# Attention rows in blocks of 128 with one block shared by two heads, and a rearranged start, in an attention-then-feed-forward kernel

## The chip, the cores and the metric

The kernel runs on one core of one Trainium2 chip. The metric is the time of one execution in microseconds of device time (us). A profile has its own span, from the first to the last instruction, which is about 2 us shorter than the time. Where differences are a few tenths of a microsecond, this document compares spans and single waits of the profiles, because the times of one kernel differ by more than that from run to run.

## The reference

```python
# q, k, v: (8 batches, 12 heads, 448 rows, 64); w_in 768 x 2048, w_out 2048 x 768
scores = q @ k.T / 8                       # per batch and head
attn = exp(scores - max) / sum
x = (attn @ v), heads side by side         # 3584 rows x 768
h = x @ w_in;  g = maximum(0.01 * h, h)
out = g @ w_out                            # float32
```

## The kernel before

Two heads of one batch make a "pair"; there are 48 pairs. TensorE (PE) forms transposed scores, ScalarE (ACT) takes exponentials into a buffer `e`, TensorE multiplies a block of rows of `e` by `v`, to which a column of ones is appended so that column 65 is the sum, VectorE (DVE) divides by it, and the result `x` is transposed into `xT` for the feed-forward layers. Attention of later pairs ("clusters") is woven between the feed-forward groups of earlier batches.

```python
SC = 112; NSC = 4                          # 448 rows = 4 blocks of 112
ps_s: 3 PSUM tiles of two banks (scores); ps_g: 2 PSUM tiles of one bank (all else)
v_sb = [v_pool.tile([SC, 2, NSC, D + 1], BF16, ...)]   # head, key chunk, 65 columns

def expo(u, c):                            # key chunk c of pair u, both heads
    e = e_sb[u % NE][:, :EL].rearrange("p (j c s) -> p j c s", j=2, c=NSC)
    nc.scalar.activation(e[:, :, c, :], sc_t.pop((u, c))[:SC, :, :S], AX.Exp, scale=scale)

def pv(u, j, bank=None):                   # head j of pair u: 16 products
    ...
    for qc in range(NSC):
        for c in range(NSC):
            at = (j * NSC + c) * S + qc * SC
            nc.tensor.matmul(ps[:, qc, :], e[:, at:at + P], vt[:, j, c, :],
                             start=(c == 0), stop=(c == NSC - 1))
    ...
    nc.vector.reciprocal(rec, ps[:SC, :, D:])
    nc.vector.tensor_mul(x_t[u][:, :, j, :], ps[:SC, :, :D], rec.to_broadcast([SC, NSC, D]))

def cluster(g):                            # r = g % 4, heads = one or two (pair, head)
    ...
    elif len(heads) > 1:
        pv(*heads.pop(0))                  # two heads: the first before the scores
    for a, c in chunks: scores(a, c)
    for a, c in chunks[:2]: expo(a, c)
    ...
    for a, j in heads:                     # one head: after the scores
        pv(a, j)
        if j == 1 and a >= NXP: x_transposes(a)     # a transposing DMA
```

This kernel loads stationary operands of 128 columns throughout, so a block of 112 rows is loaded with 16 columns of its neighbour, which are computed and thrown away.

The softmax here doesn't subtract the row's maximum and nothing guards it: scores larger than these inputs give would overflow.

Of the kernel before, what the change touches and what calls it, by code (L numbers as in the profile page):

```python
# [9 lines left out]
F32 = mybir.dt.float32  # L10
BF16 = mybir.dt.bfloat16
AX = mybir.ActivationFunctionType
# [4 lines left out]
def kernel(  # L17
# [9 lines left out]
    nc = tc.nc  # L27

    B, H, S, D = q.shape
    DM, DF = moe_w_in.shape  # L30
    P = 128
    HP = H // 2
    SC = 112
    NSC = S // SC
    KD = DM // P
    MD = DF // P
    NW = DM // 2
    NU = B * HP
    scale = 1.0 / float(D) ** 0.5
# [7 lines left out]
    ld_pool = ctx.enter_context(tc.tile_pool(name="ld", bufs=5))  # L47
# [2 lines left out]
    qk_pool = ctx.enter_context(tc.tile_pool(name="qk", bufs=1))  # L50
    exp_pool = ctx.enter_context(tc.tile_pool(name="exp", bufs=1))
    r_pool = ctx.enter_context(tc.tile_pool(name="rec", bufs=4))
    x_pool = ctx.enter_context(tc.tile_pool(name="x", bufs=3))
    xT_pool = ctx.enter_context(tc.tile_pool(name="xT", bufs=1))
    h_pool = ctx.enter_context(tc.tile_pool(name="h", bufs=2))
# [3 lines left out]
    ps_s = ctx.enter_context(tc.tile_pool(name="ps_s", bufs=3, space=PSUM))  # L59
    ps_g = ctx.enter_context(tc.tile_pool(name="ps_g", bufs=2, space=PSUM))  # L60


    NV = 5
    v_sb = [v_pool.tile([SC, 2, NSC, D + 1], BF16, name=f"v{i}") for i in range(NV)]

    NE = 3
    EL = 2 * NSC * S
    e_sb = [exp_pool.tile([SC, EL + P - SC], BF16, name=f"e{i}") for i in range(NE)]
# [6 lines left out]

    NX = 4 * S
    assert all(any(c == d for d in cuts) for c in range(0, B * S + 1, NX))
    xT = xT_pool.tile([P, KD, NX], BF16)

    w_in_sb = w_pool.tile([P, KD, DF], BF16)  # L80
    w_out_sb = w_pool.tile([P, MD, DM], BF16)
    w_in_v = moe_w_in.rearrange("(ko ki) n -> ki ko n", ki=P)
    w_out_v = moe_w_out.rearrange("(ko ki) n -> ki ko n", ki=P)

    raw = {}
    qk_sb = {}
# [3 lines left out]
    NSW = 18  # L90

    def half(t, i=None):

        t = t.rearrange("p h so d -> p (h so d)").bitcast(BF16)
        t = t.rearrange("p (u h so d) -> p u h so d", u=2, h=2, so=NSC)
        return t if i is None else t[:, i]

    def load_soft(u, n, which):
        b, hp = divmod(u, HP)
        for x in which:  # L100
            t = ld_pool.tile([SC, 2, NSC, D], F32, name="f" + "qkv"[x])
            nc.gpsimd.dma_start(
                out=half(t)[:, :n].rearrange("p u h so d -> p (u h) (so d)"),
                in_=(q, k, v)[x][b, 2 * hp:2 * hp + 2 * n].rearrange(
                    "h (p so) d -> p h (so d)", so=NSC),
            )
            for i in range(n):
                raw.setdefault(u + i, {})[x] = half(t, i)

    def load_one(u, x, queue):  # L110
        b, hp = divmod(u, HP)
        t = ld_pool.tile([SC, 2, NSC, D], F32, name="f" + "qkv"[x])
        queue.dma_start(
            out=t.rearrange("p h so d -> p h (so d)"),
            in_=(q, k, v)[x][b, 2 * hp:2 * hp + 2].rearrange("h (p so) d -> p h (so d)", so=NSC),
        )
        raw.setdefault(u, {})[x] = t

    def load(u):
        if u >= NU:  # L120
            return
        if u < NSW:
            if u % 2 == 0:
                load_soft(u, 2, (0, 1, 2))
            return
        for x in range(3):
            load_one(u, x, nc.sync)

    def cast(u, parts=(0, 1, 2), by=nc.gpsimd.tensor_copy):
        if u >= NU:  # L130
            return
        for x in parts:
            f = raw[u].pop(x)
            if u not in qk_sb:
                qk_sb[u] = cast_pool.tile([SC, 2, NSC, 2, D], BF16, name="qkb")
            if x < 2:
                by(qk_sb[u][:, x].rearrange("p so h d -> p h so d"), f)  # L137
            else:
                by(v_sb[u % NV][:, :, :, :D], f)  # L139
# [4 lines left out]
    for i in range(4):  # L144
        at = (slice(None), ts(i % 2, MD // 2), ts(i // 2, NW))
# [20 lines left out]
    warm = const_pool.tile([P, 512], BF16)  # L166
# [7 lines left out]
    def warm_up(n):  # L174
        for _ in range(n):
            ps = ps_g.tile([P, 512], F32, name="mm", tag="g")
            nc.tensor.matmul(ps, warm[:, :P], warm, start=True, stop=True)

    warm_up(8)
    for t in v_sb:  # L180
        nc.vector.memset(t[:, :, :, D:], 1.0)
# [1 line left out]
        nc.vector.memset(t[:, EL:], 0.0)  # L183
    for t in qkT:
        nc.vector.memset(t[:, QL:], 0.0)
    fast = nc.vector.tensor_copy

    cast(0, (1,), lambda o, i: (nc.scalar.copy(o[:, 0], i[:, 0]), fast(o[:, 1], i[:, 1])))
# [4 lines left out]
    x_t = {}  # L193
# [4 lines left out]
    def turn(dst, src):  # L198
        nc.sync.dma_start_transpose(out=dst.rearrange("p (c s) -> p c s", s=SC), in_=src)
# [15 lines left out]
    def transposes(u, bank=None):  # L215
        if u >= min(NPE, NU):
            return
        for parts in ((1,), (0,)) if u == 0 else ((0, 1),):
            tr = turn_tile(bank)
            for i in parts:  # L220
                for so in range(NSC):
                    nc.tensor.transpose(  # L222
                        tr[:, i, ts(so, SC)], qk_sb[u][:, i, so], ident[:SC, :SC]
                    )
            at = slice(parts[0], parts[-1] + 1)
            nc.vector.tensor_copy(  # L226
                qkT[u % NQ][:, :QL].rearrange("p (i s) -> p i s", i=2)[:, at], tr[:, at]
            )

    sc_t = {}  # L230
# [11 lines left out]
            )  # L242

    def expo(u, c):
        e = e_sb[u % NE][:, :EL].rearrange("p (j c s) -> p j c s", j=2, c=NSC)
        nc.scalar.activation(e[:, :, c, :], sc_t.pop((u, c))[:SC, :, :S], AX.Exp, scale=scale)  # L246

    def pv(u, j, bank=None):

        e, vt = e_sb[u % NE], v_sb[u % NV]  # L250
        if bank is None:
            ps = ps_g.tile([P, NSC, D + 1], F32, name="pv", tag="g")
        else:
            ps = bank[:, :NSC * (D + 1)].rearrange("p (q d) -> p q d", q=NSC)
        for qc in range(NSC):
            for c in range(NSC):
                at = (j * NSC + c) * S + qc * SC
                nc.tensor.matmul(  # L258
                    ps[:, qc, :], e[:, at:at + P], vt[:, j, c, :],
                    start=(c == 0), stop=(c == NSC - 1),  # L260
                )
        if j == 0:
            x_t[u] = x_pool.tile([SC, NSC, 2, D], BF16, name="x")
        rec = r_pool.tile([SC, NSC, 1], F32, name="rec")
        nc.vector.reciprocal(rec, ps[:SC, :, D:])  # L265
        nc.vector.tensor_mul(  # L266
            x_t[u][:, :, j, :], ps[:SC, :, :D], rec.to_broadcast([SC, NSC, D])
        )

    def x_transposes(u, bank=None):  # L270
        b, hp = divmod(u, HP)
        at = b * S % NX
        dst = xT[:, hp, at:at + S]
        if u >= NXP:
            turn(dst, x_t.pop(u).rearrange("p so h d -> p (so h d)"))
            return
        tr = turn_tile(bank)
        for so in range(NSC):
            nc.tensor.transpose(tr[:, 0, ts(so, SC)], x_t[u][:, so], ident[:SC, :SC])  # L279
        nc.vector.tensor_copy(dst, tr[:, 0, :])  # L280
# [24 lines left out]
    def part(i, m, kks, bank=None):  # L305
# [8 lines left out]
        for kk in kks:  # L314
            nc.tensor.matmul(  # L315
                open_t[m][:, :n], w_in_sb[:, kk, ts(m, P)], xT[:, kk, at:at + n],
                start=(fresh and kk == kks[0]), stop=(kk == KD - 1),
            )

    def mlp(i):  # L320
# [3 lines left out]
        if i == 0:  # L324
            for m in opened:
                part(i, m, (KD - 1,))
        for m in range(MD):
# [33 lines left out]

    def supply(u):

        for what, n in {0: [('qk', 2), ('v', 1), ('v', 2), ('load', 6)], 1: [('qk', 3), ('qk', 4), ('v', 3), ('w', 1)], 2: [('qk', 5), ('v', 4), ('v', 5), ('load', 8)], 3: [('qk', 6), ('v', 6), ('w', 1)], 4: [('qk', 7), ('v', 7), ('w', 1)], 5: [('qk', 8), ('v', 8), ('load', 10), ('w', 1)]}[u]:
            if what == "qk":
                cast(n, (0, 1), fast if n in (2, 3) else nc.gpsimd.tensor_copy)
            elif what == "v":
                cast(n, (2,))
            elif what == "load":
                load(n)  # L370
            else:
                load_w(n)

    def first(u):

        scores(u, 0)
        scores(u, 1)
        expo(u, 0)
        if u == 0:
            warm_up(2)  # L380
        expo(u, 1)
        if u == 0:
            scores(u, 2)
        if u >= 2:
            x_transposes(u - 2)
        if u >= 1:
            pv(u - 1, 0)
        if 0 < u < 2:
            scores(u, 2)
        transposes(u + 1)  # L390
        if u + 1 < HP:
            supply(u)
        if u >= 2:
            scores(u, 2)
        scores(u, 3)
        expo(u, 2)
        expo(u, 3)
        if u + 1 == HP:
            supply(u)
        if u >= 1:  # L400
            pv(u - 1, 1)


    def cluster(g):
# [35 lines left out]
    a, b = idle_slot()  # L440
# [23 lines left out]
    for i in range(B):  # L464
        work = list(range(begin[i], begin[i + 1])) if i + 1 < B else []
        n = cuts[i + 1] - cuts[i]
# [47 lines left out]
```

## Time and profile before

| | before |
|---|---|
| time, median of 3 runs | 416.49 us |
| span of the profile | 414.4 us |
| TensorE busy | 98% |
| attention-times-v products (line L258) | 1536, 13% of the chain that ended last |
| feed-forward products (L315, L349) | 70% of the chain |

The page's chain follows the work that ended last back from the end. A line with 13% there can give at most that. The lines themselves are in the prediction below.

How to read the lines of a profile: a timeline line gives the start and the duration in us, the engine, the line of kernel.py, the operation, the tile written and the tiles read, their shapes, how many instructions were merged, and in brackets how long the engine stood idle before and what ended that. PEld is TensorE's load of a stationary operand, which overlaps its products. PSUM is the memory that TensorE writes and VectorE and ScalarE read. A wait list gives total, number and longest; a DMA queue gives packets, megabytes and its share of the 16 DMA engines' time.

### The profile page before, as it was taken

The numbers are of one execution on the slowest core, as the hardware profiler recorded it, in microseconds if no ns is written. First come the engines' busy times: TensorE is split into PE (matmuls) and PEld (weight loads), VectorE is DVE, ScalarE is ACT, GpSimd is POOL, SyncE is SP. The second block draws the span as 40 slices with busy tenths as digits, with TensorE's granted clock in tenths as the row PEclk, the third lists the DMA queues.
The fourth block names the chain that finished last, engine by engine and source line by source line (L and its number), as shares of the span: only waits on it lengthen the run. The fifth ranks groups of instructions, "written<-read, shape, count | busy, mean of one in ns | idle before, by whom it ended". The sixth has DMA issues, their size and how long they took to land.

```text
span 414.4 us, 9008 instructions
## 1 busy us (share of the span) xinstructions
PE 405.9 (98%) x3758; PEld 235.8 (57%) x3758; DVE 104.0 (25%) x295; ACT 228.9 (55%) x324; POOL 105.6 (25%) x177
## 2 busy tenths in 40 slices
PE   7899999999999999999999999999999999999996
PEld 2566666554656665654565656554465666654564
DVE  3762432211323113220222212221032211320021
ACT  5988773567434774476633684467643587214300
POOL 8876656311212213130311221131130200000000
PEclk9999999999999999999999999999999999999999
DMA  9999999971866847593466947757274440230022
GB/s 133 196 201 204 202 199 129 234 186 46 178 164 175 172 114 178 140 223 100 112 161 168 205 113 182 194 149 191 77 169 132 120 58 15 60 89 0 0 78 77
DMA packets 96585, 57.23 MB, mean 138 GB/s; under 512 B 53280, under 2 KB 93088, under 8 KB 96544
## 3 DMA queue, kind: packets, MB, share of 16 engines
q1 hardware_dynamic: 76816, 44.12, 44.5%
q0 software_dynamic: 19392, 12.26, 20.6%
q8 instruction: 29, 0.48, 0.5%
q10 hardware_dynamic: 336, 0.28, 0.2%
q14 instruction: 12, 0.10, 0.1%
HBM read 45.61 MB, written 11.01 MB: 137 GB/s over the span
## 4 chain that ended last, share of the span: by engine, by line
PE 95%; DVE 2%; DMA 1%; ACT 1%; issue 0%; POOLq 0%
PE mm L349 35%; PE mm L315 35%; PE pv L258 13%; PE sc L237 10%; PE tr L222 1%; DMA fq<-in_q_dram 1%; ACT e L246 1%; PE tr L279 1%; DVE x L266 1%; PE sc L315 0%; DVE o L353 0%; DVE qkb L137 0%; DVE rec L265 0%; DVE qkT L226 0%; POOLq L498 0%
## 5 line engine op out<-in xcount | busy, mean ns | idle before, releaser
L246 ACT ACTIVATE e<-sc 112x896 bf16<-112x896 f32 x192 | 164.7, 918 | 100.1 <-PE sc L237 99.9
L349 PE MATMUL mm<-w_out_sb,h 128*128 128x384 bf16 (+1 forms) x912 | 150.2, 323 | 0.5 <-DVE x L266 0.2
L315 PE MATMUL mm<-xT,w_in_sb 128*128 128x512 bf16 (+1 forms) x756 | 148.6, 353 | 0.2 <-DVE x L266 0.2
L349 PEld LDWEIGHTS <-h 128*128 128x128 bf16 x912 | 87.0, 98 | 54.6 <-issue 0.5
L315 PEld LDWEIGHTS <-w_in_sb 128*128 128x128 bf16 x768 | 72.7, 98 | 65.5 <-issue 0.6
L330 ACT ACTIVATE h<-mm 128x512 bf16<-128x512 f32 (+1 forms) x126 | 68.8, 546 | 58.6 <-PE mm L315 58.5
L258 PEld LDWEIGHTS <-e 112*128 112x128 bf16 x1536 | 56.4, 98 | 25.7 <-issue 16.4
L139 POOL CAST v<-fv 112x512 bf16<-112x512 f32 x30 | 18.6, 618 | 194.2 <-PE pv L258 180.3
L258 PE MATMUL pv<-v,e 112*128 112x65 bf16 x1536 | 65.2, 194 | 0.2 <-ACT e L246 0.2
L353 DVE COPY o<-mm 128x384 f32<-128x384 f32 (+1 forms) x57 | 31.4, 551 | 133.5 <-PE mm L349 133.5
L265 DVE RECIPROCAL rec<-pv 112x4 f32<-112x4 f32 x96 | 17.5, 182 | 149.0 <-PE pv L258 148.4
L237 PE MATMUL sc<-qkT 64*128 64x448 bf16 x384 | 49.2, 353 | 0.9 <-DVE qkT L226 0.9
L266 DVE TENSOR_TENSOR x<-pv,rec 112x256 bf16<-112x256 f32 x96 | 40.8, 425 | 3.3
L237 PEld LDWEIGHTS <-qkT 64*128 64x128 bf16 x384 | 14.0, 94 | 18.9 <-issue 9.1
L137 POOL CAST qkb<-fk 112x512 bf16<-112x512 f32 x30 | 18.5, 616 | 1.2 <-DMA fk<-in_k_dram 1.1
L137 POOL CAST qkb<-fq 112x512 bf16<-112x512 f32 x30 | 18.5, 616 | 1.0 <-issue 1.0
L139 POOL COPY v<-fv 112x512 bf16<-112x512 bf16 x17 | 10.4, 622 | 9.4 <-DMA fv<-in_v_dram 5.6
L137 POOL COPY qkb<-fq 112x512 bf16<-112x512 bf16 x14 | 8.7, 621 | 12.8 <-DMA fq<-in_q_dram 12.8
L226 DVE COPY qkT<-tr 128x896 bf16<-128x896 bf16 (+1 forms) x15 | 8.8, 590 | 10.5 <-PE tr L222 10.4
L137 POOL COPY qkb<-fk 112x512 bf16<-112x512 bf16 x14 | 8.7, 620 | 3.6 <-DMA fk<-in_k_dram 3.5
L222 PE MATMUL tr<-ident,qkb 112*128 112x112 bf16 x112 | 8.4, 215 | 0.6 <-DVE qkb L137 0.6
L222 PEld LDWEIGHTS <-qkb 112*128 112x128 bf16 x112 | 6.9, 99 | 3.1 <-DVE qkb L137 1.2
(30 smaller groups left out, 51.6 us busy)
## 6 DMA issues: line engine op xcount, KB each, us to landing
fk<-in_k_dram SPq DMA_DIRECT2D x31, 224.0 KB, 3.4
fq<-in_q_dram SPq DMA_DIRECT2D x30, 224.0 KB, 3.2
fv<-in_v_dram SPq DMA_DIRECT2D x30, 224.0 KB, 3.8
w_in_sb<-in_moe_w_in_dram POOLq DMA_DIRECT2D x4, 768.0 KB, 11.5
w_out_sb<-in_moe_w_out_dram POOLq DMA_DIRECT2D x4, 768.0 KB, 13.8
out_dram<-o SPq DMA_DIRECT2D x7, 336.0 KB, 3.5
out_dram<-o SPq DMA_DIRECT2D x8, 288.0 KB, 2.7
out_dram<-o SPq DMA_DIRECT2D x8, 240.0 KB, 3.3
```

What stands on the lines that cost most here:

```text
L137: by(qk_sb[u][:, x].rearrange("p so h d -> p h so d"), f)
L139: by(v_sb[u % NV][:, :, :, :D], f)
L222: nc.tensor.transpose(tr[:, i, ts(so, SC)], qk_sb[u][:, i, so], ident[:SC, :SC])
L237: nc.tensor.matmul(ps[:, j, :S], t[j * D:(j + 1) * D, S + c * SC:S + c * SC + P], t[j * D:(j + 1) * D, :S], start=True, stop=True,)
L246: nc.scalar.activation(e[:, :, c, :], sc_t.pop((u, c))[:SC, :, :S], AX.Exp, scale=scale)
L258: nc.tensor.matmul(ps[:, qc, :], e[:, at:at + P], vt[:, j, c, :], start=(c == 0), stop=(c == NSC - 1),)
L265: nc.vector.reciprocal(rec, ps[:SC, :, D:])
L266: nc.vector.tensor_mul(x_t[u][:, :, j, :], ps[:SC, :, :D], rec.to_broadcast([SC, NSC, D]))
L315: nc.tensor.matmul(open_t[m][:, :n], w_in_sb[:, kk, ts(m, P)], xT[:, kk, at:at + n], start=(fresh and kk == kks[0]), stop=(kk == KD - 1),)
L330: nc.scalar.activation(h[:, m, :n], open_t.pop(m)[:, :n], AX.Prelu, alpha=0.01)
L349: nc.tensor.matmul(ps[:, :nw], h[:, m, ts(c, P)], w_out_sb[:, m, w], start=(m == 0), stop=(m == MD - 1),)
L353: nc.vector.tensor_copy(o[c][:, w], ps[:, :nw])
```

## The change

The intent is to drop products. Rows 0 to 383 of a head fill three blocks of 128, and the last 64 rows of both heads share a fourth, mixed block. The second head's q is rotated by 64 columns so that its last 64 rows stand first, right behind the first head's last 64 in `e`, which is now laid out chunk by chunk with both heads side by side. The mixed block multiplies both heads' v, and its lower half is the second head's. From pair 18 on 32 products of a pair become 28. At the start, ten small products keep TensorE busy and pair 3's casts move behind pair 0's second head.

```diff
 def expo(u, c):
-    e = ....rearrange("p (j c s) -> p j c s", j=2, c=NSC)
-    nc.scalar.activation(e[:, :, c, :], ...)
+    e = ....rearrange("p (c j s) -> p c j s", j=2, c=NSC)
+    nc.scalar.activation(e[:, c], ...)
+def pv_blocks(u, j):                       # pairs 18 to 47
+    ps = ps_g.tile([P, QB + 2, D + 1], F32, name="pv", tag="g")
+    ...                                    # products(dst, s, v): four key chunks
+    for i in range(QB):
+        products(ps[:, i, :], (S + QR) * j + i * P, vt[:, j])
+    n = QB
+    if j == 0:
+        products(ps[:, QB:, :], QB * P, vt.rearrange("p j c d -> p c j d"))
+        n = QB + 2
+    nc.vector.reciprocal(rec[:, :n], ps[:, :n, D:])
+    n = min(n, QB + 1)
+    nc.vector.tensor_mul(x[:, :n, j], ps[:, :n, :D], rec[:, :n].to_broadcast([P, n, D]))
+    if j == 0:
+        nc.vector.tensor_mul(
+            x[:QR, QB, 1], ps[QR:, QB + 1, :D], rec[QR:, QB + 1].to_broadcast([QR, D])
+        )
 ...                                        # cut: q in 3 loads and 4 casts; 128-row transposes of x
+            if u == 0:
+                stay_warm(5)               # 5 products of 128 columns, twice
-    1: [('qk', 3), ('qk', 4), ('v', 3), ('w', 1)],
+    1: [('qk', 4), ('v', 3), ('w', 1)],
+        if u == 1:                         # after pv(0, 1)
+            cast(3, (0, 1), fast)
```

More of the change, by code (lines that the diff above doesn't have):

```diff
@@ L34 @@
     NSC = S // SC
+    QB, QR = divmod(S, P)
+    assert 2 * QR == P and QR < SC
     KD = DM // P
@@ L52 @@
     r_pool = ctx.enter_context(tc.tile_pool(name="rec", bufs=4))
+    xb_pool = ctx.enter_context(tc.tile_pool(name="xb", bufs=1))
     x_pool = ctx.enter_context(tc.tile_pool(name="x", bufs=3))
@@ L77 @@
     assert all(any(c == d for d in cuts) for c in range(0, B * S + 1, NX))
-    xT = xT_pool.tile([P, KD, NX], BF16)
+    xT = xT_pool.tile([P, KD, NX + P - QR], BF16)
     w_in_sb = w_pool.tile([P, KD, DF], BF16)
@@ L83 @@
     w_out_v = moe_w_out.rearrange("(ko ki) n -> ki ko n", ki=P)
+    NXB = 3
+    xb_sb = [xb_pool.tile([P, QB + 1, 2, D], BF16, name=f"xb{i}") for i in range(NXB)]
     raw = {}
@@ L108, in load_soft, with load_q, cast_q @@
                 raw.setdefault(u + i, {})[x] = half(t, i)
+    SH = SC - QR
+    def load_q(u):
+        b, hp = divmod(u, HP)
+        t = ld_pool.tile([SC, 2, NSC, D], F32, name="fq")
+        src = [q[b, 2 * hp + h].rearrange("(p so) d -> p (so d)", so=NSC) for h in range(2)]
+        t_rows = t.rearrange("p h so d -> p h (so d)")
+        nc.sync.dma_start(out=t_rows[:, 0], in_=src[0])
+        nc.sync.dma_start(out=t_rows[QR:, 1], in_=src[1][:SH])
+        nc.sync.dma_start(out=t_rows[:QR, 1], in_=src[1][SH:])
+        raw.setdefault(u, {})[0] = t
+    def cast_q(dst, f, by):
+        by(dst[:, :, 0], f[:, 0])
+        by(dst[QR:, :, 1], f[QR:, 1])
+        by(dst[:QR, 1:, 1], f[:QR, 1, :NSC - 1])
+        by(dst[:QR, 0, 1], f[:QR, 1, NSC - 1])
     def load_one(u, x, queue):
@@ L125, in load @@
             return
-        for x in range(3):
+        load_q(u)
+        for x in (1, 2):
             load_one(u, x, nc.sync)
@@ L135, in cast @@
                 qk_sb[u] = cast_pool.tile([SC, 2, NSC, 2, D], BF16, name="qkb")
-            if x < 2:
+            if x == 0 and u >= NSW:
+                cast_q(qk_sb[u][:, 0], f, by)
+            elif x < 2:
                 by(qk_sb[u][:, x].rearrange("p so h d -> p h so d"), f)
@@ L177, in warm_up, with stay_warm @@
             nc.tensor.matmul(ps, warm[:, :P], warm, start=True, stop=True)
+    def stay_warm(n):
+        ps = ps_s.tile([P, 2, 512], F32, name="sc", tag="sc")
+        for _ in range(n):
+            nc.tensor.matmul(ps[:, 0, :P], warm[:, :P], warm[:, :P], start=True, stop=True)
     warm_up(8)
@@ L185 @@
         nc.vector.memset(t[:, QL:], 0.0)
+    for t in xb_sb:
+        nc.vector.memset(t[QR:, QB], 0.0)
     fast = nc.vector.tensor_copy
@@ L244, in expo, with products @@
     def expo(u, c):
-        e = e_sb[u % NE][:, :EL].rearrange("p (j c s) -> p j c s", j=2, c=NSC)
-        nc.scalar.activation(e[:, :, c, :], sc_t.pop((u, c))[:SC, :, :S], AX.Exp, scale=scale)
+        e = e_sb[u % NE][:, :EL].rearrange("p (c j s) -> p c j s", j=2, c=NSC)
+        nc.scalar.activation(e[:, c], sc_t.pop((u, c))[:SC, :, :S], AX.Exp, scale=scale)
+    def pv_blocks(u, j):
+        e, vt = e_sb[u % NE], v_sb[u % NV]
+        ps = ps_g.tile([P, QB + 2, D + 1], F32, name="pv", tag="g")
+        rec = r_pool.tile([P, QB + 2, 1], F32, name="recb")
+        def products(dst, s, v):
+            for c in range(NSC):
+                at = c * 2 * S + s
+                nc.tensor.matmul(
+                    dst, e[:, at:at + P], v[:, c], start=(c == 0), stop=(c == NSC - 1)
+                )
+        x_t[u] = x = xb_sb[u % NXB]
+        for i in range(QB):
[10 more added lines that the diff above has]
+                x[:QR, QB, 1], ps[QR:, QB + 1, :D], rec[QR:, QB + 1].to_broadcast([QR, D])
+            )
     def pv(u, j, bank=None):
+        if u >= NSW:
+            pv_blocks(u, j)
+            return
         e, vt = e_sb[u % NE], v_sb[u % NV]
@@ L256, in pv @@
             for c in range(NSC):
-                at = (j * NSC + c) * S + qc * SC
+                at = (c * 2 + j) * S + qc * SC
                 nc.tensor.matmul(
@@ L274, in x_transposes @@
         if u >= NXP:
-            turn(dst, x_t.pop(u).rearrange("p so h d -> p (so h d)"))
+            x = x_t.pop(u)
+            if u < NSW:
+                turn(dst, x.rearrange("p so h d -> p (so h d)"))
+                return
+            nc.sync.dma_start_transpose(
+                out=xT[:, hp, at:at + (QB + 1) * P].rearrange("p (c s) -> p c s", s=P),
+                in_=x.rearrange("p c h d -> p (c h d)"),
+            )
             return
@@ L362, in supply @@
     def supply(u):
-        for what, n in {0: [('qk', 2), ('v', 1), ('v', 2), ('load', 6)], 1: [('qk', 3), ('qk', 4), ('v', 3), ('w', 1)], 2: [('qk', 5), ('v', 4), ('v', 5), ('load', 8)], 3: [('qk', 6), ('v', 6), ('w', 1)], 4: [('qk', 7), ('v', 7), ('w', 1)], 5: [('qk', 8), ('v', 8), ('load', 10), ('w', 1)]}[u]:
+        for what, n in {0: [('qk', 2), ('v', 1), ('v', 2), ('load', 6)], 1: [('qk', 4), ('v', 3), ('w', 1)], 2: [('qk', 5), ('v', 4), ('v', 5), ('load', 8)], 3: [('qk', 6), ('v', 6), ('w', 1)], 4: [('qk', 7), ('v', 7), ('w', 1)], 5: [('qk', 8), ('v', 8), ('load', 10), ('w', 1)]}[u]:
             if what == "qk":
```

## The prediction

> **What bounds the kernel now.** I read the page's busy shares first, then the chain that ended last, then the groups by form, and last two stretches of the timeline.
>
> ```profile
> PE 405.9 (98%) x3758; PEld 235.8 (57%) x3758; DVE 104.0 (25%) x295; ACT 228.9 (55%) x324; POOL 105.6 (25%) x177
> ...
> PE 95%; DVE 2%; DMA 1%; ACT 1%; issue 0%; POOLq 0%
> PE mm L349 35%; PE mm L315 35%; PE pv L258 13%; PE sc L237 10%; PE tr L222 1%; DMA fq<-in_q_dram 1%; ACT e L246 1%; PE tr L279 1%; DVE x L266 1%; PE sc L315 0%; DVE o L353 0%; DVE qkb L137 0%; DVE rec L265 0%; DVE qkT L226 0%; POOLq L498 0%
> ```
>
> TensorE is the bound, over the whole span: 95% of the chain. The two feed-forward products (L315, L349) make 70% of it and are untouched. The change works on L258, the attention-times-v products, 13% or about 54 us for 1536 of them. VectorE and GpSimd are busy a quarter of the time, so work added there costs nothing unless it arrives late somewhere.
>
> What one product costs is not its mean duration of 194 ns, because they overlap; it is the distance from start to start. The timeline shows it:
>
> ```profile
> 258.00 0.56 DVE L353 COPY o<-mm 128x384 f32<-128x384 f32 x1 [2.04 <-PE mm L349]
> 258.41 0.74 PE L237 MATMUL sc<-qkT 64*128 64x448 bf16 x6
> 258.51 0.18 DVE L265 RECIPROCAL rec<-pv 112x4 f32<-112x4 f32 x1
> 258.73 0.42 DVE L266 TENSOR_TENSOR x<-pv,rec 112x256 bf16<-112x256 f32 x1
> 259.08 0.69 PE L258 MATMUL pv<-v,e 112*128 112x65 bf16 x16
> 259.61 2.60 PE L349 MATMUL mm<-w_out_sb,h 128*128 128x384 bf16 x15
> ```
>
> Sixteen products start at 259.08 and the next matmul at 259.61: 0.53/16 = 33 ns each. Over all 1443 neighbouring pairs of such products the start times give a mean of 32.8 ns; from the first product of an accumulation to its second it is mostly 29 ns. For wider products the chain of waits has these pieces:
>
> ```profile
> 366.51 2.76 PE mm L349 x16
> 369.27 20.72 PE mm L315 x96
> 389.99 20.86 PE mm L349 x144
> ```
>
> 96 products of 512 columns take 20.72 us, 216 ns each. The last piece is 112 products of 384 columns and 32 of 192; with 162.5 ns for 384 (from start times), the 192 take (20.86 - 18.20)/32 = 83 ns. So 512, 384 and 192 columns all fit columns/2.4 + 2.5 to 3 ns; 65 columns would be 27.1 + 2.5 = 29.6, and measure 32.8. There is a small extra of about 3 ns on the narrow product, not a floor far above its streaming time.
>
> **What the Trainium skill says.** "TensorE: Matmul & The Clock Gate", section "Wait — 56ns, not 53.3ns?", gives N / 2.4 GHz + about 2.5 ns start to start in the warm state and a floor of about 25 ns; the trace agrees at 512, 384 and 192 columns. The same page's "Back-to-back issue gap" gives about 81 ns at N=128 and 131 at N=512 for streams of weight load and matmul; this trace shows 216 at 512, so I don't use that. "SBUF — State Buffer", section "Who interferes with whom", says that a VectorE copy in a two-port mode and a GpSimd instruction block each other; the trace agrees at the start, where VectorE's 112x512 copy took 0.53 and 0.70 us while GpSimd copied v, and 0.29 at other times.
>
> **The change, part by part.**
>
> (1) Products of a pair from 18 on, 30 pairs. Before: 2 heads x 4 row blocks x 4 key chunks = 32 products of 65 columns. After: 2 x 3 x 4 = 24 of 65 columns, and 4 for the mixed block, whose stationary operand holds 64 rows of either head and which must run both heads' v past it, so 130 columns. Columns streamed: 32 x 65 = 2080 before; 24 x 65 + 4 x 130 = 2080 after. Nothing is saved in streaming; only four fixed costs go. An estimate for 130 columns: 54.2 + 2.5 = 56.7 ns. Eight products at 32.8 = 262 ns go, four at 56.7 = 227 ns come: 35.6 ns a pair, 30 pairs: -1.07 us. The last pair lies where TensorE waits for VectorE's copy of o anyway, so call it -1.03. This is all on the path.
>
> (2) VectorE. First head: a reciprocal of 5 instead of 4 columns (182 ns, mostly fixed), the same 256-column multiply (425 ns), and a new 64x64 multiply. From 425 for 256 and 182 for 4 one gets about 0.96 ns a column, so the new one is about 240 ns by estimate. Second head: 192 columns instead of 256, about -60 ns. Net +0.18 us a pair, 5 us over the kernel, on an engine idle for 310. It matters only where a PSUM buffer is awaited. In the clusters that do both heads of a pair, the sequence is first head's products, scores, second head's, feed-forward, and with two buffers the feed-forward product needs the first head's. In the stretch above VectorE is done with it at 258.73 + 0.42 = 259.15 and TensorE wants it at 259.61: 0.46 us of slack. After: the first head's products end 95 ns later (12 x 32.8 + 4 x 56.7 = 620 for 525), the new multiply adds about 0.28 with its hand-over, and TensorE arrives 36 ns earlier: 0.46 - 0.095 - 0.28 - 0.036 = 0.05 us left. So it just fits; I allow +0.1 us in all for a few misses.
>
> (3) GpSimd's q cast becomes four instructions of 256, 256, 192 and 64 columns: 768 in place of 512, at 616 ns for 512 about 0.93 us plus three more starts, some 1.1 us. The engine waits 184 us in total for L258 before its v casts, so 0.5 us more a pair is hidden. Two more load issues on SyncE at about 0.4 us each, and a transpose of 128 rows for 112: the loads run well ahead, and a pair has over 8 us. One transpose is close to its reader: the last x transpose is issued at 367.08, lands after about 2.5 us, and is wanted as the sixth product after 369.10, at 370.2. 0.6 us of slack; a longer transfer by a seventh (0.35 us) still fits. Cost 0.
>
> (4) The exponentials write 896 columns in one run instead of two of 448. ScalarE takes 917 ns for 896 elements, that is one a cycle or so; a straighter output should not change it. 0.
>
> (5) The start. From 7 to 28 us the pace is ScalarE's exponentials, 25 of them at about 0.8 us, with one hole:
>
> ```profile
> 6.96 8.19 ACT L246 ACTIVATE e<-sc 112x896 bf16<-112x896 f32 x10 [1.91 <-PE sc L237]
> 15.81 13.27 ACT L246 ACTIVATE e<-sc 112x896 bf16<-112x896 f32 x16 [0.67 <-PE sc L237]
> ...
> 12.32 0.53 DVE L137 COPY qkb<-fq 112x512 bf16<-112x512 bf16 x1
> 12.77 0.70 DVE L137 COPY qkb<-fk 112x512 bf16<-112x512 bf16 x1
> 13.39 0.16 DVE L265 RECIPROCAL rec<-pv 112x4 f32<-112x4 f32 x1
> 13.59 0.43 DVE L266 TENSOR_TENSOR x<-pv,rec 112x256 bf16<-112x256 f32 x1
> ...
> 14.07 0.37 PE L279 MATMUL tr<-ident,x 112*128 112x112 bf16 x4 [0.93 <-DVE x L266]
> ```
>
> Pair 3's casts stand in VectorE's queue before pair 0's second reciprocal; TensorE's transposes of x wait for that, later scores come late, and ScalarE idles 0.67 us. After the change, reciprocal and multiply run at about 12.7 to 13.3; the casts follow, clear of GpSimd's v copies that end at 13.3, so about 0.3 us each, to 13.95; the copy of the transposed x then frees its buffer at about 14.35, and pair 3's transposes start at 14.4, not 14.92. That brings the next scores 0.5 us forward and nearly closes the hole: -0.5 us of a possible -0.67. It is kept, because ScalarE sets the pace until 28 us and TensorE after it.
>
> (6) The ten keep-warm products of 128 columns fall in two stretches where TensorE stood for 0.8 and 0.65 us; at most 0.54 us for five in the cold state, so no delay. In this trace the clock is full from 5 us on, so nothing is gained either, though runs where it rises later may profit.
>
> Sum: -1.03 + 0.1 - 0.5 = -1.4 us: 416.5 to 415.1, a third of a per cent.
>
> **The rivals.**
>
> A: the number of weight loads decides, not the columns. If a product cost 33 ns whatever its width up to 130, 4 of 32 would go free: 4 x 32.8 x 30 = -3.9 us, with the start 412.1. For: weight loads are one to one with products, and 32.8 lies above 29.6. Against: a product of 192 columns costs 83, so the 130 wide one can't cost 33. I give it one in twenty.
>
> B: the new multiply takes more than the 0.05 us of slack. If TensorE stops 0.2 us in each of some ten feed-forward stretches where ScalarE isn't the one to free the buffer, +2 us: 416.5 to 417. For: the slack is nearly used up. Against: in the other half of the stretches no copy of o stands before the reciprocal, and each wait is short. One in six.
>
> C: the start gives nothing, as the casts now hold up pair 3's own transposes, or it gives the full 0.67 and more. Then 415.6, or 414.8.
>
> **Range and chances.** The sum's parts differ by about 0.7 us; the three times of the kernel before spread over 1.9 us, with two within 0.2. So 415.1, with 413.7 to 416.6 as eight in ten. The change is at most a per cent even under rival A, so within 2% is nearly sure.
>
> **What would show it.** Right: L258's successor lists 720 products of 65 columns and 120 of 130 for 30 pairs; a start-to-start of 55 to 60 ns for the latter; TensorE's chain share unchanged; ScalarE's hole at 15.2 us shrunk to under 0.2; no new wait of TensorE on VectorE's multiply above a few tenths in total. Wrong on (1): a mixed product at about 33 ns or above 65. Wrong on (2): the wait list names the 64x64 multiply before the feed-forward products with over 1 us. Wrong on (3): scores or feed-forward products wait for a DMA. Wrong on (5): the first exponential starts later, or the hole stays.

## The result

| | before | after |
|---|---|---|
| time, median of 6 runs | 416.70 us (416.31 to 418.94) | 416.85 us (416.49 to 417.23) |
| ratio | | 0.9991, 95% interval 0.9967 to 1.0016 |
| span of the profile | 414.39 us | 414.97 us |

A ratio is the mean time of one kernel's fast runs over that of the other's of the same rounds, so it is not quite the ratio of the medians. Executions over 1.5% slower than the fastest of the same kernel are left out of the means. No change in time is measured. The median lies 0.25 us above the predicted range, and the predicted gain of 1.4 us isn't there.

The page of the kernel after, its busy shares and chain:

```profile
PE 406.1 (98%) x3634; PEld 234.6 (57%) x3648; DVE 109.1 (26%) x328; ACT 228.7 (55%) x324; POOL 126.2 (30%) x267
...
PE 94%; DMA 3%; DVE 1%; issue 1%; POOL 1%; POOLq 0%
PE mm L432 35%; PE mm L398 34%; PE sc L277 10%; PE pv L301 8%; PE pv L333 5%; DMA fk<-in_k_dram 2%; PE tr L260 1%; DMA xT<-xb 1%; PE tr L362 1%; DVE x L341 1%; PE sc L398 0%; POOL fq L109 0%; DVE rec L340 0%; DVE o L436 0%; POOL fk L109 0%
```

TensorE still carries 94%. There is a new member with 1%, `DMA xT<-xb`: the transpose of x now stands on the path. TensorE has fewer matmuls on record, partly because 14 records are missing (768 weight loads of L398, but 742 + 12 products).

Since TensorE does the same kinds of work in the same order in both kernels, I lined up the starts of its some 250 stretches (a run of scores, of products, of one feed-forward layer) and took the differences. They account for nearly all:

| where | difference, us |
|---|---|
| the start, up to 16 us | -0.11 |
| first heads' products, pairs 18 to 46, 29 x about +108 ns | +3.15 |
| second heads' products, 29 x about -127 ns | -3.67 |
| feed-forward stretches beginning at 144.2, 241.7 and 339.1 us, 3 x 185 ns | +0.55 |
| the last batch's first feed-forward stretch, at 369.1 us | +0.62 |
| sum | +0.54 |

The span grew by 0.58 us; the remaining 0.04 are differences of a few nanoseconds each. (In the last pair, TensorE waits for VectorE's copy of o in both kernels, and nothing is gained.) So the products did save 18 ns a pair, 0.52 us in all, and the first of two new waits alone took that away. The timeline answers to the stretch in the prediction:

```profile
257.81 0.78 PE L301 MATMUL pv<-v,e 112*128 112x65 bf16 x16
258.53 0.74 PE L277 MATMUL sc<-qkT 64*128 64x448 bf16 x6
259.20 0.56 PE L301 MATMUL pv<-v,e 112*128 112x65 bf16 x12
259.60 2.76 PE L432 MATMUL mm<-w_out_sb,h 128*128 128x384 bf16 x16
```

From 259.20 to 259.60 the second head's twelve products take 0.40 us where sixteen took 0.53. The first head's stretch from 257.81 to 258.53 is 0.72 us with its four wide products (they are counted in the x16, whose printed form is that of the majority), where sixteen narrow ones took 0.61.

**The first new wait.** The kernel before near 144 us, in a block whose feed-forward groups have 384 columns:

```profile
143.70 0.68 PE L258 MATMUL pv<-v,e 112*128 112x65 bf16 x16
144.22 3.58 PE L315 MATMUL mm<-xT,w_in_sb 128*128 128x384 bf16 x21
144.42 0.18 DVE L265 RECIPROCAL rec<-pv 112x4 f32<-112x4 f32 x1 [4.55 <-PE pv L258]
144.64 0.42 DVE L266 TENSOR_TENSOR x<-pv,rec 112x256 bf16<-112x256 f32 x1
```

And the kernel after:

```profile
144.23 3.60 PE L398 MATMUL mm<-xT,w_in_sb 128*128 128x384 bf16 x20
144.43 0.20 DVE L312 RECIPROCAL recb<-pv 128x5 f32<-128x5 f32 x1 [4.72 <-PE pv L301]
144.66 0.42 DVE L314 TENSOR_TENSOR xb<-pv,recb 128x256 bf16<-128x256 f32 x1
145.09 0.23 DVE L316 TENSOR_TENSOR xb<-pv,recb 64x64 bf16<-64x64 f32 x1
145.37 2.23 PEld L398 LDWEIGHTS <-w_in_sb 128*128 128x128 bf16 x15 [0.40 <-DVE xb L316]
```

Here a single first head is followed at once by feed-forward groups of 6 products, 0.97 us each. The first group uses the other PSUM buffer; the second needs the head's own. Before, VectorE was done at 144.64 + 0.42 = 145.06. Now the 64x64 multiply ends at 145.32, and the weight load at 145.37 names it as what it waited for. The second group would have started at 144.23 + 0.97 = 145.20. As a single step of TensorE, from one product's start to the next, the wait is 335 to 336 ns where 163 is usual; the runs below are compared by that step.

**The second new wait.** The chain of the kernel after at this place, in order of time:

```profile
366.93 3.80 DMA xT<-xb
370.73 0.04 issue
370.77 0.59 PE mm L398 x2
```

The last transpose of x took 3.80 us from issue to landing; before it was issued at 367.08 and took 2.39. The packets of this stretch, first the kernel before, then after (queue, packets, megabytes, share of the stretch from 366.9 to 369.4 us):

```profile
q1 hardware_dynamic: 480, 0.11, 23.3%
```

```profile
q1 hardware_dynamic: 505, 0.12, 65.7%
q8 instruction: 1, 0.02, 3.5%
```

One packet of 16 KB from the instruction queue, from 367.9 us and 1.41 us long, runs into the transpose. Four of the transpose's 512 packets of 256 bytes then took 1.24 to 1.38 us; in the kernel before the longest took 0.04. In the kernel before the nearest such fetch came at 372.4 us.

### The profile page after: what moved, and what is told of

Same layout as the page of the kernel before. It is cut to its first block, busy times and chain, and to the rows that moved or that the text cites. A ratio compares the mean times of both kernels' runs of the same rounds, so it can differ in the third digit from the quotient of the medians.

```text
span 415.0 us, 9002 instructions
## 1 busy us (share of the span) xinstructions
PE 406.1 (98%) x3634; PEld 234.6 (57%) x3648; DVE 109.1 (26%) x328; ACT 228.7 (55%) x324; POOL 126.2 (30%) x267
## 4 chain that ended last, share of the span: by engine, by line
PE 94%; DMA 3%; DVE 1%; issue 1%; POOL 1%; POOLq 0%
PE mm L432 35%; PE mm L398 34%; PE sc L277 10%; PE pv L301 8%; PE pv L333 5%; DMA fk<-in_k_dram 2%; PE tr L260 1%; DMA xT<-xb 1%; PE tr L362 1%; DVE x L341 1%; PE sc L398 0%; POOL fq L109 0%; DVE rec L340 0%; DVE o L436 0%; POOL fk L109 0%
## 5 line engine op out<-in xcount | busy, mean ns | idle before, releaser
L398 PE MATMUL mm<-xT,w_in_sb 128*128 128x384 bf16 (+1 forms) x742 | 148.5, 352 | 1.4 <-DMA xT<-xb 0.5
L398 PEld LDWEIGHTS <-w_in_sb 128*128 128x128 bf16 x768 | 72.6, 98 | 66.7 <-DVE xb L316 1.5
L301 PEld LDWEIGHTS <-e 112*128 112x128 bf16 x840 | 33.3, 98 | 17.4 <-issue 11.5
L301 PE MATMUL pv<-v,e 112*128 112x65 bf16 (+1 forms) x840 | 40.3, 198 | 0.0
L312 DVE RECIPROCAL recb<-pv 128x5 f32<-128x5 f32 (+1 forms) x60 | 11.3, 188 | 106.7 <-PE pv L301 106.0
L333 PEld LDWEIGHTS <-e 112*128 112x128 bf16 x576 | 21.0, 98 | 8.3 <-issue 4.9
L333 PE MATMUL pv<-v,e 112*128 112x65 bf16 x576 | 24.4, 194 | 0.2 <-ACT e L286 0.2
L314 DVE TENSOR_TENSOR xb<-pv,recb 128x256 bf16<-128x256 f32 (+1 forms) x60 | 23.5, 391 | 2.1
L340 DVE RECIPROCAL rec<-pv 112x4 f32<-112x4 f32 x36 | 6.6, 182 | 37.0 <-PE pv L333 36.4
L341 DVE TENSOR_TENSOR x<-pv,rec 112x256 bf16<-112x256 f32 x36 | 15.3, 424 | 1.2
L133 POOL CAST qkb<-fq 48x256 bf16<-48x256 f32 x30 | 11.9, 398 | 2.4 <-DMA fq<-in_q_dram 0.6
```

The source lines that it names most:

```text
L301: nc.tensor.matmul(dst, e[:, at:at + P], v[:, c], start=(c == 0), stop=(c == NSC - 1))
L314: nc.vector.tensor_mul(x[:, :n, j], ps[:, :n, :D], rec[:, :n].to_broadcast([P, n, D]))
L398: nc.tensor.matmul(open_t[m][:, :n], w_in_sb[:, kk, ts(m, P)], xT[:, kk, at:at + n], start=(fresh and kk == kks[0]), stop=(kk == KD - 1),)
```

## The experiments

Eleven kernels ran, each with runs of the kernel before on the same chip. All but the seventh gave correct results. "After" below is the changed kernel.

### Moving the instruction fetch (e1)

```diff
-nc.tensor.matmul(ps, warm[:, :P], warm, start=True, stop=True)
+for i in range(4):
+    nc.tensor.matmul(ps[:, ts(i, P)], warm[:, :P], warm[:, ts(i, P)], start=True, stop=True)
```

> The changed kernel, with the eight 512-column warm-up products at the start cut into 32 of 128 columns: the same TensorE time, 48 more TensorE instructions before everything else. Theory (an instruction fetch of 16 KB, which took 1.4 us at 367.9 us on one DMA engine, held the last transpose of x, landing 3.80 us after issue): TensorE's fetches move about 48 instructions or 4 us earlier, to about 364, the last transpose lands in 2.4 us as in the kernel before, TensorE's 0.6 us wait on it is gone and the span is about 0.6 us shorter (414.4). Rival (a transpose of 128 rows is slower by itself): it lands in 3.5 to 4 us again and the wait of 0.5 to 0.6 us stays, span 415.0.

The fetch moved from 367.9 to 365.2 us, the last transpose was issued at 367.25, and it landed after 2.42 us. The stretch from 367.2 to 369.7 us holds no packet of an instruction queue:

```profile
q1 hardware_dynamic: 552, 0.15, 27.9%
xT<-xb SPq DMA_TRANSPOSE x1, 2.4
```

TensorE's wait on it is gone: between the last exponential (357.96 us before) and the last batch's first prelu (ScalarE's `maximum(0.01 * h, h)`) the kernel after had lost 0.48 us on the kernel before; this one gained 0.13. The span, 414.6 us, fell by 0.33 instead of 0.6, as a cast came late near 24 us in this run (ScalarE idle for 0.43 us). The median is 416.57 us, ratio 0.9989 (0.9965 to 1.0013). That 128-row transposes are slower by themselves is refuted: this one has 128 rows.

All thirteen profiles give the same picture. Where a fetch began 1.0 to 1.9 us after the issue of the last transpose (after, e2, e5, e6, e7, e10), it landed in 3.60 to 4.24 us; where the nearest began 1.5 to 2.1 us before it or 3.8 us or more behind it (before, e1, e3, e4, e8, e9, e11), in 2.38 to 2.42 us.

### The mixed block first (e2)

```diff
+if j == 0:
+    products(mixed block); reciprocal of its two sums; 64x64 multiply
 products(three blocks); reciprocal; large multiply
```

> The changed kernel, with the mixed block's products before the first head's other twelve, and its reciprocal and small multiply done while TensorE works on those. Theory (the 64x64 multiply of 225 ns, put behind the large one, frees the PSUM buffer too late in the three blocks of 384 columns where a single first head is followed by feed-forward groups of 0.97 us): the three waits of about 185 ns near 145, 242 and 340 us are gone, 0.55 us in all; the products themselves keep 33 and 59 ns. Rival (the waits come from something else that ends at the same time, such as ScalarE's activation): they stay. The last transpose's wait is a matter of the fetch, whose place hardly moves, so it stays at about 0.6 us or is changed by chance.

This failed, and by much: 439.1 us, ratio 1.0529 (1.0502 to 1.0555). The list of TensorE's waits (in total, times, longest) shows why, and the timeline shows one of them:

```profile
PE pv L301 <- DVE xb L310: 18.2, 30, 0.8
```

```profile
146.22 0.23 DVE L310 TENSOR_TENSOR xb<-pv,recb 64x64 bf16<-64x64 f32 x1
146.50 0.54 PE L301 MATMUL pv<-v,e 112*128 112x65 bf16 x12 [0.52 <-DVE xb L310]
```

TensorE's other twelve products write into the bank from which VectorE is reading, and the program makes them wait in each of 30 pairs. The Trainium skill knows the reason ("PSUM — Partial Sum Buffer", section "Terms": TensorE writing and VectorE reading one bank and quadrant at once is an error); I hadn't looked there. No run here lets the two overlap, so this shows only the price of keeping them apart. The experiment therefore says nothing on the three waits.

### The start of the change alone (e3)

```diff
 # the kernel before, with
+            if u == 0: stay_warm(5)
-    1: [('qk', 3), ('qk', 4), ...             # cut: the rest of the line
+    1: [('qk', 4), ...
+        if u == 1: cast(3, (0, 1), fast)
```

> The kernel before with only the start of the change: keep-warm products and pair 3's casts later. Theory: the hole in ScalarE's exponentials near 15 us (0.67 us before, 0.42 after, where pair 2's k landed 0.7 us later than before) shrinks to 0.1 to 0.2 us if the k of pair 2 lands as early as in the kernel before, and the span falls by 0.3 to 0.5 us. Second: the two runs of the kernel before above 418 us are from a clock that rises late, and the keep-warm products prevent them: all runs of this one within 0.5 us of each other. Rival: the spread has nothing to do with it, and runs above 418 us turn up here too.

Median 416.09 us, ratio 0.9975 (0.9955 to 0.9994). ScalarE's hole was 0.29 us in this profile (0.67 before, 0.42 after):

```profile
7.19 8.21 ACT L253 ACTIVATE e<-sc 112x896 bf16<-112x896 f32 x10 [2.12 <-PE sc L244]
15.68 1.73 ACT L253 ACTIVATE e<-sc 112x896 bf16<-112x896 f32 x2 [0.29 <-PE sc L244]
```

The first exponential came 0.23 us later than before, at 7.19, and the eleventh 0.13 us earlier, at 15.68; from there to the end the span stays 0.13 to 0.16 us ahead. So 0.36 us were gained from the first exponential to the eleventh, and a later start took 0.23 back: q landed 0.06 us later (5.39 against 5.33), and the transposes behind it took 0.54 us instead of 0.37, since the clock rose to full only at 6.15 us and not at 4.98. The runs spread from 415.61 to 416.37 us, more than the 0.5 expected; those of the kernel before from 415.42 to 418.04 among fast runs. Its two above 418 us are listed with mean clocks of 0.996 (418.04) and 0.999 (422.16, a slow run), so the second theory is not borne out; e11 returns to it.

### The blocks alone (e4)

```diff
 # the changed kernel, without
-            if u == 0: stay_warm(5)
 # and with pair 3's casts where they were
```

> The changed kernel without its start parts: no keep-warm products, pair 3's casts where they were. Theory: products -0.56 us, three waits +0.55 us, so no net change in the middle; ScalarE's hole is back at about 0.67 us; TensorE has 20 fewer instructions than the changed kernel at the start, so the late fetch comes some 2 us later, at about 370, after the last transpose has landed: no wait there. Span about that of the kernel before, 414.2 to 414.6. Runs above 418 us turn up as in the kernel before if the keep-warm products are what prevents them. Rival on the fetch: the wait on the last transpose stays, span 415.

Median 417.10 us, ratio 1.0003 (0.9982 to 1.0025): the blocks give nothing by themselves. The three waits (174 to 176 ns above the usual step) are there, and the last transpose landed in 2.42 us as expected, with the next fetch 5.6 us behind its issue, at 373 us and not at 370. The span of 415.0 us is longer than expected because of the start: in this profile TensorE ran at half speed until about 10 us. The same two warm-up products in the kernel before and in this one:

```profile
7.04 0.61 PE L177 MATMUL mm<-warm 128*128 128x512 bf16 x2
```

```profile
7.76 1.04 PE L207 MATMUL mm<-warm 128*128 128x512 bf16 x2
```

The exponential at 16 us came 0.56 us late, mostly by that (q also landed 0.16 us later). The hole there is 0.10 us, not 0.67, against the expectation: TensorE and ScalarE had lost the time earlier, so this run says nothing on the hole. None of its six runs, without keep-warm products, took more than 417.75 us, which speaks against the expectation that these products are what prevents runs above 418.

### A single first head before the scores (e5)

```diff
-        elif len(heads) > 1:
+        elif len(heads) > 1 or (r == 0 and heads):
```

> The changed kernel, with the single first head of a cluster put before the cluster's scores, as the clusters with two heads have it. Nothing is taken from VectorE's chain of reciprocal, large and small multiply; it gets the 0.67 us of the scores as well as one feed-forward group. Theory (the PSUM buffer of that head comes free about 0.18 us too late for the second feed-forward group of 384 columns): the three waits near 145, 242 and 340 us are gone, 0.55 us less between 119 and 358 us; no other wait is as long. Rival (the waits belong to ScalarE's prelu, whose buffer is the other of the two): they move to the first head's products and the sum stays.

Half right. VectorE's chain no longer holds TensorE there, but three waits of the same size (194 to 197 ns above the usual step) stand two feed-forward groups later, at 146.9, 244.4 and 341.8 us:

```profile
145.56 0.49 ACT L413 ACTIVATE h<-mm 128x384 bf16<-128x384 f32 x1
145.93 0.93 ACT L286 ACTIVATE e<-sc 112x896 bf16<-112x896 f32 x1
146.72 1.06 ACT L413 ACTIVATE h<-mm 128x384 bf16<-128x384 f32 x2
147.29 0.74 PEld L398 LDWEIGHTS <-w_in_sb 128*128 128x128 bf16 x5 [0.26 <-issue]
```

ScalarE's prelu activations, which empty the feed-forward buffers, now queue behind exponentials: one ends at 146.05, the next can't start before 146.72, and the feed-forward group that needs its buffer starts at 147.29, right after that one's end. (The profile itself names no releaser for this wait; this is read from the times.) Median 416.47 us, ratio 0.9982 (0.9947 to 1.0017), span 414.8. So VectorE's release is what held TensorE in the kernel after (given more time, it no longer does), but the sum of the waits stays, as the rival had it: this order of work has no 0.2 us to spare on either engine.

### v with both heads side by side (e6)

```diff
-v_sb = [v_pool.tile([SC, 2, NSC, D + 1], BF16, ...)]
+v_raw = [v_pool.tile([SC, NSC, 2, D + 1], BF16, ...)]
+v_sb = [t.rearrange("p c j d -> p j c d") for t in v_raw]
```

> The changed kernel, with v stored so that both heads' 65 columns of a key chunk lie side by side: the mixed product reads 130 columns in one run, not two of 65. Theory: its start-to-start falls from 59.0 ns to 56.7 (130/2.4 + 2.5), 0.28 us over 120 products. Rival (the extra 2.3 ns belongs to accumulation or the weight load, not to the two runs): it stays at 59. GpSimd's casts of v may change by some ns; off the path.

The mixed product hardly moved, 58.8 ns on average instead of 59.0; that guess was wrong. But the narrow products fell: in the kernel after their steps within an accumulation are mostly 29, 33, 33 and 32 ns, here 29, 34, 29 and 29. A second head's twelve take 382 ns instead of 396, and it holds in all 48 pairs. Median 415.14 us, ratio 0.9953 (0.9914 to 0.9992), span 413.4, with the three waits and a wait of 0.68 us on the last transpose still in it.

### The mixed product at half its width (e7)

```diff
-    products(ps[:, QB:, :], QB * P, vt.rearrange("p j c d -> p c j d"))
+    products(ps[:, QB, :], QB * P, vt[:, 0])          # wrong on purpose
 ...                                                   # cut: n and the small multiply follow
```

> The changed kernel, wrong on purpose: the mixed block's products take only the first head's v, 65 columns, for both heads' rows. Weight loads and instructions stay the same in number. Theory (a product costs its columns): these products cost 33 ns like the others, the 120 of them 3.1 us less, and a pair's products about 145 ns less. Rival A of the prediction (a product costs its weight load): no change, 59 ns. It also says what the change would be worth if the second head's v did not have to be streamed.

The result is wrong. The four products cost 33 ns each like the others, and a first head's sixteen take 521 ns instead of 629:

```profile
260.94 0.68 PE L301 MATMUL pv<-v,e 112*128 112x65 bf16 x16
261.46 5.36 PE L432 MATMUL mm<-w_out_sb,h 128*128 128x384 bf16 x32
```

Span 411.4 us, median 413.60, ratio 0.9916 (0.9883 to 0.9949). A product costs its columns, with the same number of weight loads; rival A of the prediction is out.

### Start and v layout without blocks (e8)

```diff
 # e3 (the kernel before with the start of the change), and
-v_sb = [v_pool.tile([SC, 2, NSC, D + 1], BF16, ...)]
+v_raw = [v_pool.tile([SC, NSC, 2, D + 1], BF16, ...)]; v_sb = rearranged views
```

> The kernel before with the start of the change and v stored with both heads' columns side by side; attention rows in blocks of 112 as before. Theory (the blocks of 128 save only 19 ns a pair and cost three VectorE waits, while the layout of v takes a first or second head's sixteen products from 522 to about 500 ns in all 48 pairs): span 414.2 of the start alone less 96 x 22 ns = 2.1 us, 412.1; about 1 us less than the run with blocks and this layout. Rival (the layout helps only next to the mixed product): span about 414.

Span 412.0 us, 2.3 less than e3. Not all of that can be put down to the layout: at the eleventh exponential, near 15 us, e8 already was 0.45 us ahead of e3, in the part of the start that varies between profiles. From there to the end it gained 1.8 us. So that the span came out as expected may be luck in part; the gain of some 20 ns a head, from 524 to 504, is not. A head's sixteen products take 0.51 us from the first to the next work:

```profile
257.22 0.67 PE L266 MATMUL pv<-v,e 112*128 112x65 bf16 x16
257.73 2.77 PE L357 MATMUL mm<-w_out_sb,h 128*128 128x384 bf16 x16
```

Median 414.32 us (413.74 to 414.49), ratio 0.9914 (0.9887 to 0.9940). It is the fastest correct kernel. Its slowest run is 0.2 us below the fastest of e9 on the same chip; e6 ran on another.

### The whole change with the v layout and the fetch moved (e9)

```diff
 # the changed kernel with the edits of e1 and e6
```

> The whole change with v side by side and the warm-up in 128-column pieces, so that the late instruction fetch misses the last transpose. Theory: the run with v side by side alone (413.4 us) less its wait of 0.68 us on the last transpose: 412.8; the three waits of 175 ns stay. Rival: the fetch's place is chance, and the wait comes back.

Span 412.7 us (expected 412.8), last transpose 2.41 us, three waits of 171 to 173 ns above the usual step. Median 414.91 us, ratio 0.9933 (0.9907 to 0.9960), 0.6 us more than e8 on the same chip. Up to the start of a feed-forward product, a first head's products take 610 ns here and a second head's 382, 992 ns a pair in blocks of 128; in e8 they take 495 and 503, 998 ns in blocks of 112. Of the blocks' gain 6 ns a pair are left, 0.2 us in all, and their three waits cost 0.5. The rest of the 0.7 us between the two spans lies in the start: e9 is 0.2 us behind e8 at 11 us.

### The changed kernel again (e10)

> The changed kernel itself once more, for a second profile and for times on the same chip as the other two. Theory: the fetch of instructions is tied to the count of instructions, so it lies at 367.5 to 368.5 us again and the last transpose lands 3.6 to 4 us after issue; three waits of about 185 ns; clock 0.998 or more in every run. Rival (the late landing was an accident of one run): it lands in 2.4 us.

The fetch lay at 368.4 us, the transpose landed after 4.02 us, and TensorE waited 0.84 us for it; the three waits were 175 to 176 ns above the usual step. Span 415.3, median 416.87 us, ratio 0.9977 (0.9948 to 1.0006), while the kernel before spread from 416.53 to 419.65 us on this chip. The late landing is a property of the kernel, not an accident.

### The keep-warm products alone (e11)

```diff
 # the kernel before, with
+            if u == 0: stay_warm(5)
```

> The kernel before with the ten keep-warm products alone; pair 3's casts stay where they were. Theory: no run with a mean clock under 0.998 (in the runs so far 11 of 35 without the keep-warm products lay under 0.997, none of 50 with them), so the median falls by a few tenths against the kernel before; ScalarE's hole near 15 us stays at about 0.6 to 0.7 us, so the profiled span is about 414.4, that of the kernel before. Rival (the moved casts bring the whole gain of the start part): low clocks turn up, and the median is that of the kernel before.

Median 416.60 us, ratio 0.9995 (0.9974 to 1.0015). One run of six had a mean granted clock of 0.996 and took 418.43 us, so the claim that they rule out low clocks is wrong. Over all timed runs whose clock is listed, 1 of 56 with keep-warm products lay under 0.997, and 12 of 46 without: it is rarer, in runs on several chips. But the listed mean says little of a late rise. It counts only what is on record, and a profile's record begins when the clock rises: e4's profiled run is listed at 1.000 though its clock rose at 10.17 us, and e6's 0.998 comes from the end, where the record falls to half at 411.9 us, 1.5 us before the last instruction. Nor does it explain the slow runs: of the 11 among 40 runs of the kernel before that took over 418 us, 7 are listed at 0.998 or more. What sets them apart stays open.

ScalarE's hole was 0.53 us, against 0.29 with the moved casts as well (e3); so most of the shrinking goes with the casts. The gain of e3 can't be split cleanly, since the arrival of the first loads and the rise of the clock move the start by up to 0.8 us between profiles (first exponential at 6.77 to 7.60 us).

## Why the prediction was right or wrong

**Class and bound: right.** TensorE's products stay the bound, and the change is far within 2%. That was nearly sure from the size of every term and says little for the steps. The sum of -1.4 us was wrong; the balance of the profiles is +0.58. Of the signs that the prediction set for itself, the product counts (720 and 120) and the 59 ns came out right; the hole stayed above 0.2 us, the new waits on the multiply exceed a few tenths, a feed-forward product waits for a DMA, and the first exponential starts later.

**(1) Products: the mechanism right, the size half.** The columns decide, as e7 shows, and only fixed costs go. But two terms of the 35.6 ns were mis-sized. The wide product takes 59.0 ns, not 56.7: 9 ns a pair. And the average of 32.8 ns that I applied to the products removed holds the slower first two steps of each head (38 and 36 ns) and the waits; a removed accumulation of four costs 29 + 33 + 33 + 32 = 127 ns, not 131, twice a pair. Measured: -18 ns a pair, 0.52 us, not 1.03.

**(2) VectorE: wrong in its last sentence.** The two-head clusters, whose slack I worked out as 0.05 us, indeed held. The multiply took 225 ns, near the estimate of 240. What failed is the step "I allow +0.1 us in all": I had looked only at clusters with two heads, and the single first head before groups of 384 columns has less time, one group of 0.97 us. Three waits of 185 ns, +0.55 us. This is rival B in another place and with a quarter of its size.

**(3) The transpose: wrong.** "0.6 us of slack ... Cost 0" rested on a landing of 2.5 us plus a seventh for the rows. The rows cost nothing visible (2.42 us in e1), but the changed count of instructions moved a fetch into it: 3.80 us, and 0.62 us on the path. e1 and e10 show it both ways. I had the queue of instructions on the page and left it out of the reckoning.

**(4) Exponentials: right.** 916 ns on average, 917 before.

**(5) The start: mechanism right, size not.** The hole shrank from 0.67 to 0.42 us, not to 0.12. Pair 2's k landed at 11.58 us instead of 10.86 in this profile, so TensorE lost 0.44 us to it that it had not lost before, and the first exponential came 0.14 us late. -0.1 us was left of -0.5 at the eleventh exponential. The traces of all ten profiles with the moved casts show how the two go together: the hole is 0.42 us where pair 2's k landed 4.5 us or more after the first exponential (after, e1, e7, e10), 0.36 at 4.4 (e2), 0.29 at 4.1 (e3), and at most 0.1 at 3.4 to 4.3 (e5, e6, e8, e9). In the two that kept the casts where they were and had the clock by 7 us (before, e11) it is 0.67 and 0.53, though k landed 3.9 and 3.8 after. So moving the casts opened the way, and the arrival of k then decided, with e3 not quite in line. That arrival varies between profiles with the same start, and nothing here shows what sets it. One figure of the prediction was read too narrowly: VectorE's copies at other times took 0.29 to 0.40 us, not 0.29 alone; the moved ones took 0.28 and 0.29.

**(6) Keep-warm products: right for this profile; the side remark is not shown.** No delay, no gain where the clock rose at 5 us. Runs with a low mean clock are rarer with them, but that mean leaves out a late rise (e11). In the eleven profiles with these products the clock rose between 4.7 and 7.0 us, in the two without at 5.0 and 10.2; two are too few to tell.

Open is why the layout of v makes the narrow products faster. That it does is shown by e6, e8 and e9; both heads' products show the same steps, though their columns begin at different offsets.

## What to carry to other kernels

Count the columns that TensorE streams before counting its instructions: merging two half blocks that need different moving operands saves only the fixed few nanoseconds of each product (here 18 ns for four). TensorE is 98% busy here, so an instruction added behind a PSUM buffer must be held against the shortest work that follows any of its uses (one group of 0.97 us), not against the typical one. And when a DMA lands just before the bound engine needs it, look where the instruction fetches lie: a change elsewhere in the program moves them.

## What the Trainium skill lacked or had wrong

- "TensorE: Matmul & The Clock Gate", "Back-to-back issue gap": 131 ns a matmul at N=512 in a stream with weight loads. These runs show 216 ns at 512, 59 at 130 and 29 to 33 at 65, each with its own weight load.
- The same page's N / 2.4 + 2.5 ns (29.6 for 65 columns) knows no layout of the streamed operand. Narrow products of 65 columns took mostly 29, 33, 33 and 32 ns with one layout of v and 29, 34, 29 and 29 with the other, 1.8 us from 15 us to the end (e8 against e3); no page has it.
- "Runtime: NRT & Kernel Launch", "Instruction fetch mechanics", has the fetch itself, in blocks of 16 KiB over a DMA queue. No page says what a fetch costs a transfer that it meets. The packets took 0.9 to 2.1 us, 28 in the kernel after, and six of six that began 1.0 to 1.9 us after the issue of the last transpose put its landing at 3.6 to 4.2 us, against 2.4.
